# Turning q and k by DMA transposes in SBUF instead of TensorE transposes and bank copies, in a windowed attention followed by a mixture of experts

## The chip, the cores and the metric

The kernel runs on one core of one Trainium2 chip. The metric is the device time of one execution in microseconds (us); less is better. A verdict needs 2%: faster, same or slower.

## The reference, cut to what matters

```python
# q, k, v: (4 batches, 8 heads, 768 tokens, 64), float32; n_sink = 4, window = 128
scores = scale * q @ k.T
keep = is_sink | ((rel >= 0) & (rel < window))      # first 4 keys, and the last 128
a = softmax(where(keep, scores, -1e9))
x = (a @ v) as (3072 tokens, 512)                   # 4 x 768 tokens, 8 heads x 64
# a mixture of 4 experts, dense: every token goes through every expert
p = domain_probs / sum(domain_probs)
out = sum over e of p[:, e] * (relu(x @ w1[e]) @ w2[e])   # 512 -> 1024 -> 512
```

## The kernel before

The expert products are most of the work. Attention of batch b+1 is woven into the expert products of batch b, by a small model of the engines' times that the kernel carries in its Python: it decides the program's order when the kernel is built. At run time TensorE keeps to that order: it stands before a step that has to wait, even with products behind it that are ready.

The score products of this kernel read q and k with the head dimension on the partitions (`sps<-qkT 64*128` in the page). Before, each batch is loaded with tokens on the partitions, cast to bf16 on the way, regrouped by head, turned by TensorE into a PSUM bank (12 transposes for a pair of heads), and copied out of the bank:

```python
def load_qk(b, piece):                       # one DMA each for q and k, T tokens per partition
    s0, T = PIECES[b][piece]
    ...
        nc.gpsimd.dma_start(out=x, in_=src[b, :, s0:s0 + P * T, :]
                            .rearrange("h (p t) d -> p h (t d)", t=T))   # T = 6: runs of 1536 bytes

def transposes(b, piece, hp, tag="mix"):
    ...
    for i, name in enumerate("qk"):
        for tt in range(T):
            nc.tensor.transpose(tr[:, i, tt], nat[b, piece, name][:, tt, 2 * hp:2 * hp + 2, :], ident)
    done = pe(2 * T * P, grouped[b, piece], free_at(tag))
    engine, at = sooner(2 * T * P, done, rate=0.9)
    copy(engine, qkT[b, hp][:, :, s0:s0 + T * P].rearrange("c i (p t) -> c i p t", t=T),
         tr.rearrange("c i t p -> c i p t"))
    ...
```

The main loop starts the next batch's attention when the present one is done. `load_w1(3)` and `load_w2(3)` bring the last expert's weights, 1 MB each as written:

```python
        if not att.more() and ahead + 1 < B and (ahead == 0 or mix.done >= cols * ahead):
            ahead += 1
            load_qk(ahead, 0)
            load_v(ahead, range(NQB))
            if ahead == 1:
                load_w1(3)
                load_w2(3)
            att = Attention(ahead, [("regroup", ahead, 0, 0)]
                + [("transposes", ahead, 0, hp) for hp in range(NHP)]
                + [("sinks", ahead, 0, 0)], range(NG))
```

`sinks` is the first step that reads the turned q and k: GpSimd makes the sink keys (`ksd`) from the turned k, then TensorE multiplies them with the turned q.

The softmax here doesn't subtract the row's maximum and nothing guards it: scores larger than these inputs give would overflow.

Of the kernel before, what the change touches and what calls it, by code (L numbers as in the profile page):

```python
# [12 lines left out]
BF16 = mybir.dt.bfloat16  # L13
# [3 lines left out]
def kernel(  # L17
# [12 lines left out]
    nc = tc.nc  # L30

    B, H, S, D = q.shape
    NSINK = int(n_sink)
# [4 lines left out]
    P = 128  # L38
# [6 lines left out]
    NQB = S // P  # L45
    NHP = H // 2
# [28 lines left out]
    def act(cols, *deps):  # L75
        t["act"] = max(t["act"], *deps) + 190 + cols / 1.2
        return t["act"] + 60

    def dve(cols, *deps, rate=0.96):
        t["dve"] = max(t["dve"], *deps) + 130 + cols / rate  # L80
        return t["dve"] + 60
# [12 lines left out]
    def lands(key, nbytes):  # L94
        dma["at"] += nbytes / 350.0
        landed[key] = dma["at"] + 1500
# [9 lines left out]



    nat = {}

    def load_qk(b, piece):
        s0, T = PIECES[b][piece]
        for name, src in (("q", q), ("k", k)):
            x = sb.tile([P, H, T * D], BF16, name=f"{name}n", tag=f"{name}n", bufs=1)
            nc.gpsimd.dma_start(
                out=x, in_=src[b, :, s0:s0 + P * T, :].rearrange("h (p t) d -> p h (t d)", t=T),
            )
            nat[b, piece, name] = x
        lands(("qk", b, piece), 2 * H * P * T * D * 4)

    def load_first():

# [11 lines left out]
    def copy(engine, out, in_):  # L134
        (nc.scalar.copy if engine == "act" else nc.vector.tensor_copy)(out=out, in_=in_)  # L135

    def sooner(cols, *deps, rate=0.96):

        a = max(t["act"], *deps) + 190 + cols / 1.2
        d = max(t["dve"], *deps) + 130 + cols / rate  # L140
        if a <= d:
            return "act", act(cols, *deps)
        return "dve", dve(cols, *deps, rate=rate)
# [134 lines left out]
        for _ in range(n):  # L278
            nc.tensor.matmul(x[:, 0:cols], lhsT=zeros[:, 0:P], rhs=zeros[:, 0:cols], start=True, stop=True)

    qkT, xT, sinkA, aTs, onats = {}, {}, {}, {}, {}
    turned_at, sinkA_at, aT_at, onat_at, xT_at = {}, {}, {}, {}, {}

    def two_banks(tag="mix"):

# [5 lines left out]
    def transposes(b, piece, hp, tag="mix"):  # L291

        s0, T = PIECES[b][piece]
        if (b, hp) not in qkT:
            qkT[b, hp] = sb.tile([P, 2, S], BF16, name="qkT", tag="qkT", bufs=5)
        tr = psum.tile([P, 2, T, P], BF16, name="tr", tag=tag, bufs=1 if tag == "mix" else 2)
        for i, name in enumerate("qk"):
            for tt in range(T):
                nc.tensor.transpose(tr[:, i, tt], nat[b, piece, name][:, tt, 2 * hp:2 * hp + 2, :], ident)  # L299
        done = pe(2 * T * P, grouped[b, piece], free_at(tag))  # L300
        engine, at = sooner(2 * T * P, done, rate=0.9)
        copy(
            engine, qkT[b, hp][:, :, s0:s0 + T * P].rearrange("c i (p t) -> c i p t", t=T),
            tr.rearrange("c i t p -> c i p t"),
        )
        take(tag, at)
        turned_at[b, piece, hp] = at

    def sink_keys(b):
        for hp in range(NHP):  # L310
            nc.gpsimd.tensor_mul(  # L311
                ksd[b % 2][:, hp, 0:2 * NSINK].rearrange("p (a j) -> p a j", a=2),
                qkT[b, hp][:, 1, None, 0:NSINK].to_broadcast([P, 2, NSINK]),
                half[:, :, None].to_broadcast([P, 2, NSINK]),
            )

    def sink_values(b):
        nc.gpsimd.tensor_mul(
            vsd[:, b], vsf[:, b, None, None, :].to_broadcast([P, NHP, 2, DX]), sel2,
        )  # L320

    def sinks(b, piece):

        if b not in sinkA:
            sinkA[b] = sb.tile([P, 2 * G], BF16, name="sinkA", tag="sinkA", bufs=2)
        s0, T = PIECES[b][piece]
        q0, q1 = max(G, s0), s0 + T * P
        sp, _ = two_banks()
        for hp in range(NHP):
            nc.tensor.matmul(  # L330
                sp[0][32 * hp:32 * hp + 32, 0:q1 - q0], lhsT=ksd[b % 2][:, hp, :],
                rhs=qkT[b, hp][:, 0, q0:q1], start=True, stop=True,
            )
        nc.scalar.activation(
            out=sinkA[b][:, q0 - G:q1 - G], in_=sp[0][:, 0:q1 - q0], func=AF.Exp, scale=scale,
        )
        done = pe(q1 - q0 + 300, free_at("mix"), *[turned_at[b, piece, hp] for hp in range(NHP)])
        at = act(q1 - q0, done)
        take("mix", at)
        for g in range(q0 // G, q1 // G):  # L340
            sinkA_at[b, g] = at

    def scores(b, hp, g, tag="mix"):
        T = qkT[b, hp]
        w = sum(x[2] for x in GROUPS[g]) * P
        sps, both = two_banks(tag)
        c = 0
        for (kb, qb, nq) in GROUPS[g]:
            for ph in range(2):
                pr = slice(64 * ph, 64 * ph + 64)  # L350
                nc.tensor.matmul(  # L351
                    sps[ph][:, c:c + nq * P],
                    lhsT=T[pr, 1, kb * P:(kb + 1) * P],
                    rhs=T[pr, 0, qb * P:(qb + nq) * P],
                    start=True, stop=True,
                )
            c += nq * P
        done = pe(1.5 * w, scores_ready(b, hp, g, tag))
        a = sb.tile([P, 2, w], BF16, name="aT", tag="aT", bufs=4)
        m = mask0 if g == 0 else mask1  # L360
        if both is not None:
            nc.scalar.activation(out=a, in_=both[:, :, 0:w], func=AF.Exp, scale=scale)  # L362
            nc.vector.tensor_mul(a, a, m[:, None, :].to_broadcast([P, 2, w]))  # L363
            at = act(2 * w, done)
            take(tag, at)
            at = dve(2 * w, at, rate=1.9)
        else:
            for ph in range(2):
                nc.scalar.activation(out=a[:, ph], in_=sps[ph][:, 0:w], func=AF.Exp, scale=scale)
                nc.vector.tensor_mul(a[:, ph], a[:, ph], m)  # L370
                at = act(w, done)
                take(tag, at)
                at = dve(w, at, rate=1.9)
        aTs[b, hp, g], aT_at[b, hp, g] = a, at
# [64 lines left out]
    class Attention:  # L439
# [29 lines left out]
        def emit(self, step):  # L469
            self.steps += 1  # L470
            if step == "turn":
                turn(*self.valued.pop(0))
            elif step == "values":
                u = self.scored.pop(0)
                values(*u)
                self.valued.append(u)
            else:
                kind, b, x, y = self.todo.pop(0)
                if kind == "scores":
                    scores(b, x, y)  # L480
                    self.scored.append((b, x, y))
                elif kind == "regroup":
                    regroup(b, x)
                    if b > 0:
                        sink_values(b)
                elif kind == "transposes":
                    transposes(b, x, y)
                elif kind == "sinks":
                    if b > 0:
                        sink_keys(b)  # L490
                    sinks(b, x)


# [147 lines left out]
    while mix.more() or att.more():  # L641
        now = t["pe"]

        if not att.more() and ahead + 1 < B and (ahead == 0 or mix.done >= cols * ahead):
            ahead += 1
            load_qk(ahead, 0)
            load_v(ahead, range(NQB))
            if ahead == 1:
                load_w1(3)
                load_w2(3)  # L650
            att = Attention(
                ahead, [("regroup", ahead, 0, 0)] + [("transposes", ahead, 0, hp) for hp in range(NHP)]
                + [("sinks", ahead, 0, 0)], range(NG),
            )
            upto = mix.done
        share = (cols * ahead - upto) * 0.96
        due = ahead == 0 or att.steps * share <= (mix.done - upto) * att.total
        opts = []
        if att.more():
            opts = [(max(r, now), 0 if due else 3, "att", step) for r, step in att.options()]  # L660
        f, s2 = mix.first_ready(), mix.second_ready()
        opts.append((max(f, now), 2, "first", None))
        opts.append((max(s2, now), 1 if mix.since >= 2 else 2.5, "second", None))
        r, _, kind, step = min(opts, key=lambda o: (o[0] > now + 40, o[0] if o[0] > now + 40 else 0, o[1]))
        if kind == "att":
            att.emit(step)
        elif kind == "first":
            mix.emit_first()
        else:
            mix.emit_second()  # L670
# [35 lines left out]
```

## Time and profile before

| | before |
|---|---|
| time, median of the first three runs | 420.56 us (419.39 to 420.58) |
| span of the profiled run | 417.9 us |
| TensorE busy | 398.6 us, 95% |
| ScalarE / VectorE busy | 188.7 us / 176.0 us |
| TensorE transposes of q and k | 192 |

The page of the kernel before: each engine's busy time with its share of the span and its instructions, then the span in 40 slices (10.4 us each, busy tenths; PEclk is the granted TensorE clock in tenths).

```profile
PE 398.6 (95%) x2874; PEld 229.3 (55%) x2918; DVE 176.0 (42%) x349; ACT 188.7 (45%) x336; POOL 50.1 (12%) x94
...
PE   6598899999999999999999999999999999999996
...
PEclk9599899999999999999999999999999999999999
DMA  9999999292011129200002100000001100000012
```

TensorE is full from the sixth slice on. All its holes lie in the first five, in batch 0's attention, and so does its half clock, but for the last of it, which ends at 53.4 us. Whatever is taken from TensorE after that should shorten the kernel by as much (e8 below tests it).

What one group of 12 transposes costs is read from the timeline of TensorE before (start in us, length, engine, line, operation, operands, count). The lengths overlap (68.53 + 0.50 lies past the next start, 68.87), so starts count: from 68.53 to the next product's 69.20 it is 0.67 us.

```profile
68.53 0.50 PE L299 MATMUL tr<-ident,qo 128*128 128x128 bf16 x6
68.87 0.50 PE L299 MATMUL tr<-ident,ko 128*128 128x128 bf16 x6
69.20 2.15 PE L547 MATMUL hps<-xT,w 128*128 128x256 bf16 x16
```

The hole at the end of batch 0's attention, and the first long run of expert products after it, in the timeline of TensorE before:

```profile
48.92 0.29 PE L402 MATMUL od<-vx,aT 128*128 128x65 bf16 x4 [1.33 <-DVE aT L363]
...
50.39 6.10 PE L547 MATMUL hps<-xT,w 128*128 128x256 bf16 x36
```

Two windows of 1 us of the kernel before (columns: length, then busy time and instructions of PE, PEld, DVE, ACT, POOL; clock; DMA share; GB/s written). In the first, q and k are read in runs of 1536 bytes, in the second v in runs of 256. (These are float32 in HBM; cast to bf16 they are written as packets of 768 and 128 bytes.)

```profile
86.00:87.00 1.00, 1.00 (x14) 0.60 (x13) 0.26 (x1) 0.15 (x1) 1.00 (x2) 1.00 1.33 199
...
92.00:93.00 1.00, 0.95 (x6) 0.41 (x6) 0.46 (x3) 0.95 (x2) 0.00 (x0) 1.00 2.43 155
```

### The profile page before, as it was taken

What the parts mean: (1) busy time and instruction counts of PE and PEld (TensorE: products, weight loads), DVE (VectorE), ACT (ScalarE), POOL (GpSimd) and SP (SyncE); (2) the same over time, 40 slices, a digit from 0 to 9 for tenths busy, and PEclk for the clock granted to TensorE, in tenths of its full rate; (3) what the DMA queues carried; (4) which work ended last, traced back from release to release, by engine and by line L of the source; (5) the groups of instructions that cost most, each with busy time, mean ns of one, the idle gap of its engine ahead of it and who ended that gap; (6) DMA issues with size and microseconds to landing.
All of it is one profiled execution on the core that took longest, in us unless ns stands there. A gap on an engine that the chain in (4) does not pass through costs nothing.

```text
span 417.9 us, 7002 instructions
## 1 busy us (share of the span) xinstructions
PE 398.6 (95%) x2874; PEld 229.3 (55%) x2918; DVE 176.0 (42%) x349; ACT 188.7 (45%) x336; POOL 50.1 (12%) x94
## 2 busy tenths in 40 slices
PE   6598899999999999999999999999999999999996
PEld 2366566666676555555555555555555555555552
DVE  3666655565564446343333444334334222222222
ACT  3556315473641554445544645355534333333331
POOL 8745120440000044000000000000000000000000
PEclk9599899999999999999999999999999999999999
DMA  9999999292011129200002100000001100000012
GB/s 175 191 194 209 206 182 164 28 184 17 2 41 61 52 28 184 18 0 2 0 2 77 76 2 0 2 0 2 2 0 56 72 27 0 2 0 2 0 51 100
DMA packets 47428, 25.16 MB, mean 60 GB/s; under 512 B 29965, under 2 KB 42253, under 8 KB 47397
## 3 DMA queue, kind: packets, MB, share of 16 engines
q0 software_dynamic: 41632, 17.30, 33.4%
q1 hardware_dynamic: 5764, 7.42, 5.1%
q8 instruction: 22, 0.36, 0.3%
q14 instruction: 10, 0.07, 0.1%
HBM read 35.73 MB, written 6.29 MB: 101 GB/s over the span
## 4 chain that ended last, share of the span: by engine, by line
PE 91%; DMA 3%; ACT 2%; POOL 1%; DVE 1%; issue 1%; ACTq 0%
PE hps L547 41%; PE mop L582 39%; PE sps L351 3%; DMA kn<-in_k_dram 3%; PE tr L299 3%; PE od L402 2%; PE tx L427 1%; ACT aT L362 1%; PE od L395 1%; POOL vx L177 0%; ACT qkT L135 0%; DVE ht L558 0%; PE sps L330 0%; DVE aT L363 0%; ACT ko L135 0%
## 5 line engine op out<-in xcount | busy, mean ns | idle before, releaser
L547 PE MATMUL hps<-xT,w 128*128 128x384 bf16 (+1 forms) x1152 | 195.6, 310 | 0.5
L582 PE MATMUL mop<-w,ht 128*128 128x512 bf16 x724 | 174.5, 379 | 3.3 <-issue 1.4
L556 ACT ACTIVATE ht<-hps 128x384 bf16<-128x384 f32 (+1 forms) x222 | 103.0, 470 | 149.3 <-PE hps L547 148.3
L547 PEld LDWEIGHTS <-w 128*128 128x128 bf16 x1152 | 108.2, 98 | 62.3 <-issue 8.4
L582 PEld LDWEIGHTS <-ht 128*128 128x128 bf16 x768 | 73.0, 98 | 77.8 <-issue 2.7
L592 DVE SCALAR_TENSOR_TENSOR out_sb<-mop,scale_t,out_sb 128x512 f32<-128x512 f32 x72 | 54.0, 750 | 106.9 <-PE mop L582 105.8
L363 DVE TENSOR_TENSOR aT<-aT,mask 128x1024 bf16<-128x1024 bf16 (+1 forms) x46 | 31.2, 678 | 50.9 <-ACT aT L362 50.7
L362 ACT ACTIVATE aT<-sps 128x1024 bf16<-128x1024 f32 (+1 forms) x46 | 44.0, 957 | 12.6 <-PE sps L351 12.4
L558 DVE TENSOR_SCALAR ht<-hps 128x256 bf16<-128x256 f32 (+1 forms) x66 | 29.8, 451 | 18.9 <-PE hps L547 16.9
L590 DVE TENSOR_SCALAR out_sb<-mop,scale_t 128x512 f32<-128x512 f32 x24 | 18.0, 750 | 34.9 <-PE mop L582 34.8
L135 ACT COPY qkT<-tr 128x1536 bf16<-128x1536 bf16 (+1 forms) x20 | 21.9, 1098 | 16.5 <-PE tr L299 16.5
L135 ACT COPY xT<-tx 128x256 bf16<-128x256 bf16 x32 | 11.9, 374 | 26.6 <-PE tx L427 26.0
L311 POOL TENSOR_TENSOR ksd<-qkT,half 128x8 bf16<-128x8 bf16 x16 | 3.1, 203 | 170.0 <-ACT qkT L135 170.0
L402 PE MATMUL od<-vx,aT 128*128 128x65 bf16 x352 | 20.9, 197 | 2.4 <-DVE aT L363 2.4
L177 POOL DMA_DIRECT2D vx<-in_v_dram x24 | 21.3, 915 | 9.8 <-DMA w<-in_moe_w_dram 9.8
L402 PEld LDWEIGHTS <-aT 128*128 128x128 bf16 x352 | 17.8, 100 | 6.8 <-DVE aT L363 3.2
L412 DVE TENSOR_TENSOR onat<-od,R 128x256 bf16<-128x256 f32 x48 | 20.4, 424 | 1.7
L351 PE MATMUL sps<-qkT 64*128 64x128 bf16 (+1 forms) x256 | 18.4, 246 | 0.5
L427 PE MATMUL tx<-ident,onat 128*128 128x128 bf16 x96 | 13.7, 228 | 3.7 <-DVE onat L412 3.0
L427 PEld LDWEIGHTS <-onat 128*128 128x128 bf16 x96 | 8.3, 99 | 11.5 <-DVE onat L412 4.7
L351 PEld LDWEIGHTS <-qkT 64*128 64x128 bf16 x256 | 8.0, 96 | 10.9 <-issue 9.1
L395 PE MATMUL od<-vsd,sinkA 128*128 128x130 bf16 x64 | 12.9, 220 | 0.0
(60 smaller groups left out, 119.4 us busy)
## 6 DMA issues: line engine op xcount, KB each, us to landing
w<-in_moe_w_dram POOLq DMA_DIRECT2D x8, 1024.0 KB, 15.3
out_dram<-out_sb SPq DMA_DIRECT2D x24, 256.0 KB
vx<-in_v_dram POOLq DMA_DIRECT2D x24, 128.0 KB, 10.9
qn<-in_q_dram POOLq DMA_DIRECT2D x3, 768.0 KB, 7.8
kn<-in_k_dram POOLq DMA_DIRECT2D x3, 768.0 KB, 10.9
qraw<-in_q_dram SPq DMA_DIRECT2D x2, 256.0 KB
kraw<-in_k_dram SPq DMA_DIRECT2D x2, 256.0 KB
qn<-in_q_dram POOLq DMA_DIRECT2D x2, 256.0 KB, 9.9
```

The source lines that it names most:

```text
L135: (nc.scalar.copy if engine == "act" else nc.vector.tensor_copy)(out=out, in_=in_)
L177: nc.gpsimd.dma_start(out=vx[b % 2][:, tb, :, 0:D], in_=v[b, :, tb * P:(tb + 1) * P, :].rearrange("h p d -> p h d"),)
L351: nc.tensor.matmul(sps[ph][:, c:c + nq * P], lhsT=T[pr, 1, kb * P:(kb + 1) * P], rhs=T[pr, 0, qb * P:(qb + nq) * P], start=True, stop=True,)
L362: nc.scalar.activation(out=a, in_=both[:, :, 0:w], func=AF.Exp, scale=scale)
L363: nc.vector.tensor_mul(a, a, m[:, None, :].to_broadcast([P, 2, w]))
L402: nc.tensor.matmul(od[:, qi, ph], lhsT=a[:, ph, c:c + P], rhs=vx[b % 2][:, kb, 2 * hp + ph, 0:DX], start=(g == 0 and i == 0), stop=(i == l ...
L427: nc.tensor.transpose(tx[:, qi], o[:, qi], ident)
L547: nc.tensor.matmul(hp_, lhsT=w1_sb[e][:, db, fb * P:(fb + 1) * P], rhs=xT[b, db][:, t0:t0 + n], start=(db == 0), stop=(db == NDB - 1),)
L556: nc.scalar.activation(out=ht, in_=hp_, func=AF.Relu)
L558: nc.vector.tensor_scalar(out=ht, in0=hp_, scalar1=0.0, scalar2=None, op0=ALU.max)
L582: nc.tensor.matmul(op, lhsT=hts[fb][:, off:off + P], rhs=w2_sb[e][:, fb, :], start=(fb == 0), stop=(fb == NFB - 1),)
L592: nc.vector.scalar_tensor_tensor(out=dst, in0=op, scalar=sc, in1=dst, op0=ALU.mult, op1=ALU.add,)
```

## The change

The intent is to take 144 transposes off TensorE, and 12 bank copies and the regroupings of batches 1 to 3 off ScalarE and VectorE, by giving the turning to the DMA engines, which are mostly idle after the first 70 us (31 of the last 33 slices of the page before show 0 to 2 tenths). q and k of these batches are loaded by blocks of 128 tokens (six loads each), and one DMA transpose each writes them turned into SBUF. Batch 0 keeps TensorE, but its turned q and k move to the new layout, and each bank copy is split over ScalarE and VectorE. The diff, cut to its core (the uses of `qkT[b, hp]` become uses of `qkT[b][..., hp, :]`):

```diff
+    def load_rows(b):
+        for i, (name, src) in enumerate((("q", q), ("k", k))):
+            x = sb.tile([P, NQB, H, D], BF16, name=f"{name}n", tag=f"{name}n", bufs=1)
+            for tb in range(NQB):
+                nc.gpsimd.dma_start(
+                    out=x[:, tb], in_=src[b, :, tb * P:(tb + 1) * P, :].rearrange("h p d -> p h d"),
+                )
+                lands(("rows", b), H * P * D * 4)
+            if b not in qkT:
+                qkT[b] = sb.tile([P, 2, NQB, NHP, P], BF16, name="qkT", tag="qkT", bufs=2)
+            nc.sync.dma_start_transpose(
+                out=qkT[b][:, i].rearrange("c t h p -> c (t h) p"),
+                in_=x.rearrange("p t h d -> p (t h d)"),
+            )
+        for hp in range(NHP):
+            turned_at[b, 0, hp] = max(landed["rows", b], t["pe"]) + 11000.0
...
     def transposes(b, piece, hp, tag="mix"):            # batch 0 only, now
-        engine, at = sooner(2 * T * P, done, rate=0.9)
-        copy(engine, qkT[b, hp][:, :, s0:s0 + T * P]..., tr...)
+        for i, engine in enumerate(("act", "dve")):
+            copy(engine, qkT[b][:, i, s0 // P:s0 // P + T, hp, :]..., tr[:, i]...)
+        at = max(act(T * P, done), dve(T * P, done, rate=0.9))
...
-            load_qk(ahead, 0)
+            load_rows(ahead)
             load_v(ahead, range(NQB))
             if ahead == 1:
                 load_w1(3)
                 load_w2(3)
             att = Attention(
-                ahead, [("regroup", ahead, 0, 0)] + [("transposes", ahead, 0, hp) for hp in range(NHP)]
-                + [("sinks", ahead, 0, 0)], range(NG),
+                ahead, [("sinks", ahead, 0, 0)], range(NG),
             )
```

The 11000 is nanoseconds: where the scheduler's model expects the transposes to be done. It places TensorE's sink scores in the program, it does not make anything wait less.

More of the change, by code (lines that the diff above doesn't have):

```diff
@@ L105 @@
     ctx.enter_context(tc.manual_schedule())
-    nat = {}
+    nat, qkT, turned_at = {}, {}, {}
     def load_qk(b, piece):
@@ L279, in idle_products @@
             nc.tensor.matmul(x[:, 0:cols], lhsT=zeros[:, 0:P], rhs=zeros[:, 0:cols], start=True, stop=True)
-    qkT, xT, sinkA, aTs, onats = {}, {}, {}, {}, {}
-    turned_at, sinkA_at, aT_at, onat_at, xT_at = {}, {}, {}, {}, {}
+    xT, sinkA, aTs, onats = {}, {}, {}, {}
+    sinkA_at, aT_at, onat_at, xT_at = {}, {}, {}, {}
     def two_banks(tag="mix"):
@@ L293, in transposes @@
         s0, T = PIECES[b][piece]
-        if (b, hp) not in qkT:
-            qkT[b, hp] = sb.tile([P, 2, S], BF16, name="qkT", tag="qkT", bufs=5)
+        if b not in qkT:
+            qkT[b] = sb.tile([P, 2, NQB, NHP, P], BF16, name="qkT", tag="qkT", bufs=2)
         tr = psum.tile([P, 2, T, P], BF16, name="tr", tag=tag, bufs=1 if tag == "mix" else 2)
@@ L300, in transposes @@
         done = pe(2 * T * P, grouped[b, piece], free_at(tag))
-        engine, at = sooner(2 * T * P, done, rate=0.9)
-        copy(
-            engine, qkT[b, hp][:, :, s0:s0 + T * P].rearrange("c i (p t) -> c i p t", t=T),
-            tr.rearrange("c i t p -> c i p t"),
-        )
+        for i, engine in enumerate(("act", "dve")):
+            copy(
+                engine, qkT[b][:, i, s0 // P:s0 // P + T, hp, :].rearrange("c n (p t) -> c n p t", t=T),
+                tr[:, i].rearrange("c t (n p) -> c n p t", n=T),
+            )
+        at = max(act(T * P, done), dve(T * P, done, rate=0.9))
         take(tag, at)
@@ L312, in sink_keys @@
                 ksd[b % 2][:, hp, 0:2 * NSINK].rearrange("p (a j) -> p a j", a=2),
-                qkT[b, hp][:, 1, None, 0:NSINK].to_broadcast([P, 2, NSINK]),
+                qkT[b][:, 1, 0, hp, None, 0:NSINK].to_broadcast([P, 2, NSINK]),
                 half[:, :, None].to_broadcast([P, 2, NSINK]),
@@ L331, in sinks @@
                 sp[0][32 * hp:32 * hp + 32, 0:q1 - q0], lhsT=ksd[b % 2][:, hp, :],
-                rhs=qkT[b, hp][:, 0, q0:q1], start=True, stop=True,
+                rhs=qkT[b][:, 0, q0 // P:q1 // P, hp, :], start=True, stop=True,
             )
@@ L343, in scores @@
     def scores(b, hp, g, tag="mix"):
-        T = qkT[b, hp]
+        T = qkT[b]
         w = sum(x[2] for x in GROUPS[g]) * P
@@ L352, in scores @@
                     sps[ph][:, c:c + nq * P],
-                    lhsT=T[pr, 1, kb * P:(kb + 1) * P],
-                    rhs=T[pr, 0, qb * P:(qb + nq) * P],
+                    lhsT=T[pr, 1, kb, hp, :],
+                    rhs=T[pr, 0, qb:qb + nq, hp, :],
                     start=True, stop=True,
@@ L483, in emit @@
                     regroup(b, x)
-                    if b > 0:
-                        sink_values(b)
                 elif kind == "transposes":
@@ L490, in emit @@
                         sink_keys(b)
+                        sink_values(b)
                     sinks(b, x)
```

## The prediction

> **What bounds the kernel now.** TensorE. The busy table has it at 398.6 of 417.9 us (95%), and the chain of waits runs 91% through its instructions. From about 56 us on it practically never waits; its idle time (the 40 slices and a table of 2 us windows) lies before that, in batch 0's attention, where it also runs at half clock from about 9 to 22.5 us and, after a hole at 47.4 to 50.2 us, from 50 to 53.4 us. ScalarE (45%) and VectorE (42%) are no limits after that.
>
> **What goes, what comes.** For batches 1 to 3 the change removes:
> - TensorE: 12 groups of 12 transposes. In the timeline one group takes 0.67 us from its start to the next product's start (68.53 to 69.20, 149.75 to 150.42): 12 x 0.67 = 8.0 us, all on the path, since TensorE is saturated there.
> - ScalarE: 12 bank copies of 1.44 us, and the regroupings on ScalarE and VectorE: about 25 us of engine time, worth almost nothing.
>
> It adds, per batch, 12 loads with 256-byte runs in place of two with 1536-byte runs. The 1 us windows show v, with such short runs, at 155 GB/s written (91 to 94 us), against 200 to 206 for q and k (84 to 89): 1.57 MB takes an estimated 10.1 us in place of 7.8. For batches 2 and 3 this happens a whole batch ahead (loads issue at 80 and 153 us): free. For batch 1 the weights in front end near 49.7 us, so k should land near 61 us; what needs it stands near 75 us in the new order.
>
> It adds two DMA transposes of 786 KB per batch, in the SP queue behind output stores. For batches 2 and 3 they cannot start before the fifth store of the former batch, and the new order puts the sink scores that need them only about 10 us of TensorE work later. [...] TensorE waits 0 to 2 us at batches 2 and 3, none at batch 1.
>
> Batch 0 keeps its transposes, but each copy is split over ScalarE and VectorE (0.59 or 0.69 us become an estimated 0.4 us on both); each bank then waits for both in-order engines, and the third piece's transposes move later. I count +0.5 us.
>
> **Sum.** 420.6 - 8.0 + 0.5 + about 0.4 of waits: **413.5 us**, 80% range **409.5 to 422**. Chances: faster by over 2% 0.30, within 2% 0.58, slower 0.12.
>
> **What would show it.** Transposes on TensorE 192 -> 48, its busy time down by about 8 us, ScalarE's by about 20 us; no wait of the sink scores over 2 us; SP's queue with six transposes whose pairs land 8 to 11 us after issue; q and k loaded at about 155 GB/s; TensorE still saturated from 56 us on.
>
> **What would make it wrong.** DMA transposes much slower than 200 GB/s: TensorE, in order, then stands at the sink scores of batches 2 and 3, each hole costing its length and some 1.7 us of half clock after it (as after the hole at 47 us)[...]. Or batch 1's loads or transposes slowed by the v and w loads around them. Or the hole at 47 us going with the new order of batch 0: 2 us better.

The sum came to 413.5 us, with the four terms that it shows. The 200 GB/s of the last paragraph are a condition of the forecast; measured were 200 to 206 GB/s for the loads of q and k before, and 270 for a transpose alone.

## The result, and the profile after

| | before | after |
|---|---|---|
| time, median of 4 runs | 420.25 us | 431.92 us (430.65 to 432.80) |
| ratio | | 1.028 (1.025 to 1.031): slower |
| span of the profiled run | 417.9 us | 431.1 us |
| TensorE / ScalarE busy | 398.6 / 188.7 us | 398.3 / 169.4 us |

The same lines of the page, after (slices of 10.8 us):

```profile
PE 398.3 (92%) x2774; PEld 223.2 (52%) x2774; DVE 168.1 (39%) x348; ACT 169.4 (39%) x331; POOL 76.0 (18%) x124
...
PE   7599799049999999999999999999999999999996
...
PEclk9599889759999999999999999999999999999999
DMA  9999999999800159910000180000001110000012
```

There is a new hole in the eighth and ninth slice with half clock behind it, and the DMA engines are busy through it. Everything later is full. The waits of TensorE after (who waited for whom: total us, times, longest) name it, and GpSimd's own wait says what stood behind it:

```profile
PE sps L349 <- POOL ksd L330: 15.7, 1, 15.7
...
POOL ksd L330 <- DMA qkT<-kn: 162.5, 3, 77.7
```

It is one wait: of three batches with DMA transposes, one has it. (GpSimd's 162.5 us are harmless; it has nothing else to do.) The timeline of TensorE after shows where:

```profile
51.75 6.80 PE L565 MATMUL hps<-xT,w 128*128 128x256 bf16 x36
...
74.98 1.04 PE L565 MATMUL hps<-xT,w 128*128 128x256 bf16 x8
91.70 1.08 PE L349 MATMUL sps<-qkT,ksd 128*32 128x512 bf16 x4 [15.69 <-POOL ksd L330]
92.71 3.59 PE L600 MATMUL mop<-w,ht 128*128 128x512 bf16 x8
```

The sink scores of batch 1 stood at 76 us in the program, as predicted, and ran at 91.70. The eight products after them took 3.59 us in place of 1.89: half clock. The timeline of the SP queue after has the six transposes (the length is the time that SP was held by issuing it; the output stores between the pairs are left out):

```profile
54.92 7.41 SPq L132 DMA_TRANSPOSE qkT<-qn  x1
62.57 15.10 SPq L132 DMA_TRANSPOSE qkT<-kn  x1
...
155.86 3.04 SPq L132 DMA_TRANSPOSE qkT<-qn  x1
159.13 3.06 SPq L132 DMA_TRANSPOSE qkT<-kn  x1
...
250.87 3.10 SPq L132 DMA_TRANSPOSE qkT<-qn  x1
254.21 2.93 SPq L132 DMA_TRANSPOSE qkT<-kn  x1
```

The same instruction took 2.9 to 3.1 us to issue at batches 2 and 3 and 7.4 and 15.1 us at batch 1, and what lay behind it in the queue waited: a store whose data was ready at 158.17 us was issued at 162.29, after batch 2's pair. In the chain of waits after (start, length, what), the stretch before the hole is one transfer:

```profile
62.57 28.74 DMA qkT<-kn
```

The trace also has every DMA packet with its queue, start and size. Counted in stretches of 2 us, q0 being the loads issued by GpSimd and q1 the transposes (256-byte packets, 3072 for q and as many for k):

```
kernel after            q0 loads                        q1 transposes
60 to 62 us    255 x 128 B                              927 x 256 B  119 GB/s
68 to 70 us    1081 x 128 B                             560 x 256 B   72 GB/s
74 to 76 us    132 x 128 B and 44 x 2048 B              174 x 256 B   22 GB/s
82 to 84 us    39 x 1024 B and 82 x 2048 B              124 x 256 B   16 GB/s
158 to 159 us (1 us, batch 2)   none                   1132 x 256 B  290 GB/s
```

In the five stretches from 80 to 90 us, beside packets of 1024 and 2048 bytes only, the transposes moved 16 to 34 GB/s. By its packets, k of batch 1 was turned from 68.0 to 90.9 us: 22.8 us. k of batch 2, with no load beside it, took 2.9 us (160.3 to 163.2). And the last expert's weights suffered in return: their packets run from 71.5 to 93.9 us, against 59.9 to 72.0 us before.

Three reasons could stand behind this:
- **A**: the long packets of the weight loads, beside which the transposes starve.
- **B**: the short packets of v and of the late q and k rows; the weights do not matter.
- **C**: the first DMA transposes of a program are slow by themselves.

And a second, smaller loss was there before the hole: the run of 36 expert products starts at 51.75 us in place of 50.39 and takes 6.80 us in place of 6.10, at half clock for 6.8 us in place of 3.4.

### The profile page after: what moved, and what is told of

Its sections match the earlier page's. It is cut to its first block, busy times and chain, and to the rows that moved or that the text cites. A ratio compares the mean times of both kernels' runs of the same rounds, so it can differ in the third digit from the quotient of the medians. Undisturbed runs are those within 1.5% of the kernel's fastest.

```text
span 431.1 us, 6810 instructions
## 1 busy us (share of the span) xinstructions
PE 398.3 (92%) x2774; PEld 223.2 (52%) x2774; DVE 168.1 (39%) x348; ACT 169.4 (39%) x331; POOL 76.0 (18%) x124
## 4 chain that ended last, share of the span: by engine, by line
PE 77%; DMA 17%; POOL 4%; DVE 0%; issue 0%; ACT 0%; ACTq 0%; DVEq 0%; POOLq 0%
PE mop L600 36%; PE hps L565 35%; DMA w<-in_moe_w_dram 9%; DMA qkT<-kn 7%; PE sps L370 3%; PE od L421 2%; POOL vx L195 2%; DMA vx<-in_v_dram 1%; POOL kn L126 1%; PE tx L446 1%; PE od L414 1%; PE sps L349 0%; DVE ht L576 0%; POOL kn L115 0%; POOL qn L115 0%
## 5 line engine op out<-in xcount | busy, mean ns | idle before, releaser
L574 ACT ACTIVATE ht<-hps 128x384 bf16<-128x384 f32 (+1 forms) x234 | 109.2, 471 | 188.5 <-PE hps L565 187.2
L600 PE MATMUL mop<-w,ht 128*128 128x512 bf16 x768 | 183.0, 382 | 0.0
L565 PEld LDWEIGHTS <-w 128*128 128x128 bf16 x1152 | 109.4, 99 | 66.5 <-issue 9.4
L382 DVE TENSOR_TENSOR aT<-aT,mask 128x1024 bf16<-128x1024 bf16 (+1 forms) x46 | 30.0, 652 | 39.8 <-ACT aT L381 39.5
L330 POOL TENSOR_TENSOR ksd<-qkT,half 128x8 bf16<-128x8 bf16 x16 | 2.7, 196 | 162.5 <-DMA qkT<-kn 162.5
L576 DVE TENSOR_SCALAR ht<-hps 128x256 bf16<-128x256 f32 (+1 forms) x54 | 23.1, 429 | 11.1 <-PE hps L565 9.3
L126 POOL DMA_DIRECT2D qn<-in_q_dram x18 | 15.9, 904 | 10.0 <-DVE R L428 8.1
L126 POOL DMA_DIRECT2D kn<-in_k_dram x18 | 15.9, 926 | 8.5 <-ACT aT L381 4.3
L349 PE MATMUL sps<-qkT,ksd 128*32 128x512 bf16 (+1 forms) x20 | 2.5, 390 | 15.7 <-POOL ksd L330 15.7
L153 ACT COPY xT<-tx 128x256 bf16<-128x256 bf16 x25 | 9.1, 373 | 16.6 <-PE tx L446 16.0
```

The lines of the kernel that those rows point to most:

```text
L126: nc.gpsimd.dma_start(out=x[:, tb], in_=src[b, :, tb * P:(tb + 1) * P, :].rearrange("h p d -> p h d"),)
L382: nc.vector.tensor_mul(a, a, m[:, None, :].to_broadcast([P, 2, w]))
L565: nc.tensor.matmul(hp_, lhsT=w1_sb[e][:, db, fb * P:(fb + 1) * P], rhs=xT[b, db][:, t0:t0 + n], start=(db == 0), stop=(db == NDB - 1),)
L574: nc.scalar.activation(out=ht, in_=hp_, func=AF.Relu)
L576: nc.vector.tensor_scalar(out=ht, in0=hp_, scalar1=0.0, scalar2=None, op0=ALU.max)
L600: nc.tensor.matmul(op, lhsT=hts[fb][:, off:off + P], rhs=w2_sb[e][:, fb, :], start=(fb == 0), stop=(fb == NFB - 1),)
```

## The experiments

All eight gave the reference's result. The first four shared one chip and seven runs of the kernel before (420.90 us), the other four another and seven runs (420.40 us).

### e1_w3_after: the last weights after the transposes

```diff
-            if ahead == 1:
-                load_w1(3)
-                load_w2(3)
...
                     if b > 0:
                         sink_keys(b)
                         sink_values(b)
+                    if b == 1:
+                        load_w1(3)
+                        load_w2(3)
```

> The changed kernel, but the last expert's two weight loads (2.1 MB written) are issued only once batch 1's transposes have landed. Theory A (the transposes of batch 1 share the DMA engines packet by packet with those weight loads, and starve): k's transpose of batch 1 lands before 72 us in place of 91 us, the 15.7 us wait of TensorE at batch 1's sink scores is under 1 us, and the time falls by that wait and the half clock behind it, about 18 to 19 us, to 413 us (411.5 to 415). Theory B (the short-run loads of k and v slow the transposes, the weights do not matter): k's transpose still lands after 80 us and at least 6 us of the wait stay: 420 or more. Theory C (the first transposes are slow by themselves, whatever runs beside them): nothing changes, 431 us.

Measured: 415.95 us (415.65 to 416.48), ratio 0.989 (0.987 to 0.991). TensorE's wait for the sink keys, in its waits of this run:

```profile
PE sps L349 <- POOL ksd L330: 0.3, 1, 0.3
```

k was turned by 75.7 us (its packets), not before 72 as A had it, as v's short packets still ran beside it until 73.8; but the wait is gone. B and C both asked for a wait that stays, so as they were stated they fall: without the weights there is no loss. The time came down by 16 us, of which the wait is 15.4. A's forecast of 413 missed by 3 us, though its saving came: from the 101st product of the first expert layer (in every kernel just after batch 0's attention) to the last one, TensorE needs 343.4 us in place of 361.4, 18.0 less. But e1 reaches that 101st product 0.9 us later than the changed kernel (60.97 against 60.11), for which no run shows the cause, and the changed kernel's profiled run, from which the wait was read, took 432.8 us, 0.9 more than its median.

### e2_v_first: v out of the way, the weights beside the transposes

```diff
-            load_rows(ahead)
-            load_v(ahead, range(NQB))
+            if ahead == 1:
+                load_v(ahead, range(NQB))
+                load_rows(ahead)
+            else:
+                load_rows(ahead)
+                load_v(ahead, range(NQB))
```

> The changed kernel, but batch 1's v is loaded before its q and k, so that v is out of the way when k is transposed and only the weight loads run beside it; q and k land about 5 us later. Theory A (weights): k's transpose still lands at 88 us or later and TensorE waits 10 us or more: 427 to 437 us. Theory B (v and the other short-run loads): the wait falls below 6 us and the time below 422 us.

Measured: 416.41 us (415.68 to 417.57), ratio 0.990. A said 427 to 437 and is wrong as well. B's forecast for this run (a wait under 6 us, a time under 422) is met, but e1 had already ruled B out:

```profile
PE sps L349 <- POOL ksd L330: 1.4, 1, 1.4
```

The packets say why. Beside the weights the transposes did starve, just as A has it: from 66 to 68 us 179 load packets, nearly all of 2048 bytes, and exactly 179 transpose packets, 23 GB/s. But the weights lost little: 181 GB/s in that stretch, and 14.8 us for all of them (62.2 to 77.0) against 12.1 before. Then the transposes ran at 274 GB/s and were done at 81.1. (The scheduler had also moved the sink scores about 4.5 us later, to 80.5 us, since it counts v's bytes as coming first. With the old place the wait would have been an estimated 6 us: 1.4 plus 4.5.) So neither kind of load alone makes the 15.7 us: with v alone (e1) k was turned at 75.7 us, with the weights alone at 81.1 (though the transposes began 5.8 us later there, at 64.0), with both at 90.9. That asks for a theory of what passes between the two queues; e7 tests one.

### e3_te_batch1: batch 1 turned by TensorE

```diff
+            if b == 1:                       # in load_rows: no DMA transpose
+                nat[b, 0, name] = x
+                continue
...
-                ahead, [("sinks", ahead, 0, 0)], range(NG),
+                ahead, ([("transposes", 1, 0, hp) for hp in range(NHP)] if ahead == 1 else [])
+                + [("sinks", ahead, 0, 0)], range(NG),
```

> The changed kernel with batch 1 alone turned by TensorE again (rows loaded as in the change, 48 transposes, bank copies split over two engines); batches 2 and 3 by DMA. If the loss is all in batch 1's hole (A and B alike), the hole and its half clock go (about 19 us) and 4 x 0.67 = 2.7 us of transposes return: 415.5 us (414 to 418). If the DMA transposes of batches 2 and 3 or batch 0's split copies cost much too, it stays above 420.

Measured: 417.59 us (416.92 to 418.32), ratio 0.993. It lies in the range. The DMA transposes of batches 2 and 3 are a gain, and the row loads (which this run keeps) are not the loss. It also speaks against C: here batch 2's are the first DMA transposes of the program, and by its packets the first of them took 3.1 us.

### e4_later_sinks: the same transfers, met later

```diff
-            turned_at[b, 0, hp] = max(landed["rows", b], t["pe"]) + 11000.0
+            turned_at[b, 0, hp] = max(landed["rows", b], t["pe"]) + (28000.0 if b == 1 else 11000.0)
```

> The changed kernel with one number of its scheduler changed: batch 1's turned q and k are expected 28 us after the load step in place of 11 us, so TensorE gets batch 0's expert products first and meets batch 1's sink scores near 92 us. If what costs is only TensorE standing in order before a late transpose, the wait falls below 3 us although the transpose lands as late as before (85 us or later): 413 to 416 us. If the slow transposes also hold back something else that TensorE needs (the last expert's weights, v), waits appear there instead and it stays above 420 us.

Measured: 415.14 us (413.99 to 415.39), ratio 0.987. Here the transfers are as slow as in the changed kernel (k turned at 90.3 us, the weights done at 94.2), but TensorE's timeline has the sink scores without a wait (the first line is GpSimd's, in its own timeline):

```profile
90.92 0.67 POOL L330 TENSOR_TENSOR ksd<-qkT,half 128x8 bf16<-128x8 bf16 x4 [29.21 <-DMA qkT<-kn]
...
92.60 0.40 PE L349 MATMUL sps<-qkT,ksd 128*32 128x512 bf16 x4
```

The slow transfers cost nothing that shows by themselves (e1, without them, took 415.95). What cost was TensorE, in order, standing in front of them while expert products that were ready lay behind in its program.

### e5_one_copy: e1 with batch 0's bank copies on one engine each

```diff
-        for i, engine in enumerate(("act", "dve")):
+        engine, at = sooner(2 * T * P, done, rate=0.9)
+        for i in range(2):
             copy(engine, qkT[b][:, i, s0 // P:s0 // P + T, hp, :]..., tr[:, i]...)
-        at = max(act(T * P, done), dve(T * P, done, rate=0.9))
```

> The run with the last weights after the transposes (415.95 us), with batch 0's bank copies each put back on one engine. In that run the 65th product of the first expert layer started at 52.4 us against 50.4 before, and half clock lasted 6.8 us from 51 us against 3.4. If the split copies made that, it starts at 50.5 to 51 us here and the time is 413.5 to 414.5 us. If the strided bank copies of the new layout or the row loads beside them made it, it stays at 415.5 to 416.5 us.

Measured: 413.99 us (413.40 to 414.52), ratio 0.985. The time is as the split copies' theory has it, 2.0 us under e1. The milestone is not: the 65th product starts at 51.5 us, not by 51. What did shrink is the half clock after it, 3.4 us again in place of 6.8 in this profile.

### e6_before_split: that part of the change alone

The kernel before, with nothing changed but batch 0's bank copies:

```diff
-        engine, at = sooner(2 * T * P, done, rate=0.9)
-        copy(engine, qkT[b, hp][:, :, s0:s0 + T * P]..., tr...)
+        if b == 0:
+            for i, engine in enumerate(("act", "dve")):
+                copy(engine, qkT[b, hp][:, i, s0:s0 + T * P]..., tr[:, i]...)
+            at = max(act(T * P, done), dve(T * P, done, rate=0.9))
+        else:
+            ...                              # as before
```

> The kernel before with one part of the change alone: batch 0's bank copies split over ScalarE and VectorE, in the old layout, and the order that the scheduler makes of it. If that part costs what the milestones say, 422 to 423 us (1.5 to 2.5 us over before). If it costs nothing, 420.3 to 421.2 us.

Measured: 421.88 us (421.75 to 422.45), ratio 1.0039 (1.0024 to 1.0054): 1.5 us over before, just under the forecast's 422. The split, with the order that the scheduler makes of it, costs about 1.5 to 2 us, and it does so without DMA transposes.

### e7_short_w3: the weights in short packets

```diff
-                load_w1(3)                   # one load, runs of 1024 elements
-                load_w2(3)                   # one load, runs of 512 elements
+                for c in range(0, F, 256):   # four loads, runs of 256 elements (512 bytes)
+                    nc.gpsimd.dma_start(out=w1_sb[3][:, :, c:c + 256], in_=...[:, :, c:c + 256])
+                for c in range(0, Dout, 256):    # two loads
+                    nc.gpsimd.dma_start(out=w2_sb[3][:, :, c:c + 256], in_=...[:, :, c:c + 256])
```

> The changed kernel with the last expert's weights loaded in runs of 512 bytes in place of 2048 and 1024 (six loads in place of two), in the same place of the queue, still after v. Theory D (packets take turns, so a 256-byte transpose packet gets an eighth of the bytes of a 2048-byte one beside it): the transposes move 60 GB/s or more beside these weights in place of 16 to 34, k lands at 82 us or before, and TensorE waits under 7 us: 416 to 423 us. Theory E (it is the mixture of three kinds of traffic in flight that collapses, whatever the length): k lands after 87 us and the wait stays over 11 us: 427 us or more.

Measured: 421.67 us (421.39 to 421.99), ratio 1.0032. The same bytes in the same place of the queue, cut into packets a quarter (w1) or half (w2) as long, and the wait of TensorE is under a third:

```profile
PE sps L349 <- POOL ksd L330: 4.7, 1, 4.7
```

k was turned at 80.5 us. From 78 to 80 us the trace has 449 packets of 512 bytes and 449 of 256: turn by turn, 115 and 57 GB/s. The turns can be seen one by one: packets of one kind start in a bunch of about 16, then as many of the other, and the pattern comes back every 67 ns. Landing, wait and time are as D has them, and E falls. (The rate was just under D's 60 GB/s there; from 76 to 78 us, where the traffic changes, it was 29.)

### e8_apart: nothing beside the transposes

The edits of e1, e2 and e5 together.

> Nothing beside batch 1's transposes: v before q and k, the last weights after the transposes, and batch 0's copies on one engine. If contention is all that slowed them, the two transposes land within 9 us of k's last load, as those of batches 2 and 3 do, TensorE waits under 1 us for them, and the time is 412.5 to 414.5 us: the saved 8.0 us of TensorE work less what is still lost in batch 0.

Measured: 413.18 us (412.85 to 413.63), ratio 0.983 (0.982 to 0.985): the best of all, better than both kernels, though short of 2%. The SP queue of this run, and the sink keys and sink scores in the timelines of GpSimd and TensorE:

```profile
60.97 5.76 SPq L132 DMA_TRANSPOSE qkT<-qn  x1
66.96 3.98 SPq L132 DMA_TRANSPOSE qkT<-kn  x1
...
73.01 0.67 POOL L330 TENSOR_TENSOR ksd<-qkT,half 128x8 bf16<-128x8 bf16 x4 [12.24 <-DMA qkT<-kn]
...
81.58 0.40 PE L349 MATMUL sps<-qkT,ksd 128*32 128x512 bf16 x4
```

k's packets end at 72.4 us; GpSimd made the sink keys at 73.0 us and TensorE came to them at 81.6 without a wait. C falls here too: by their packets the two transposes took 5.2 us (k's last rows still landed beside the first) and 4.2 us. That is slower than the 2.9 to 3.4 us of batches 2 and 3, which no run explains, but far from the 22.8 us of k in the changed kernel. In the same profile, from the 101st product of the first expert layer to the last, TensorE needs 342.7 us (59.15 to 401.80) against 350.4 before (58.05 to 408.47): 7.7 of the 8.0 us that the transposes were said to be worth. At the 101st product it is still 1.1 us behind. The new layout's two small copies for each large one may be the cause, or the clock: in this profile the first half-clock spell lasts 17.1 us against 13.7 before, and none follows the hole. No run parts the two.

## Why the prediction was wrong

- **TensorE bounds the kernel; 144 transposes are worth 8.0 us.** Right. e8 has 7.7 us of it. That TensorE's busy time would fall by 8 us did not show in the changed kernel (398.6 to 398.3), because products at half clock are busy for longer (eight took 3.59 us in place of 1.89), and because the trace before lacks 44 of 768 records of the second expert product; in two runs with all records it is 401.8 (e6, all transposes on TensorE) and 394.3 (e8).
- **ScalarE falls by about 20 us, worth nothing.** Right: 188.7 to 169.4.
- **Loads in 256-byte runs at 155 GB/s, k in near 61 us.** Right: 155 GB/s, and k's transpose was issued at 62.57.
- **A pair of transposes takes 8 to 11 us and just fits at batches 2 and 3.** Right: from the first issue to the sink keys 8.0 us (155.86 to 163.82) and 8.2 us (250.87 to 259.09), and no wait. Each transpose took 2.9 to 3.1 us by its packets (k of batch 2: 786 KB in 2.91 us, 270 GB/s).
- **"TensorE waits 0 to 2 us at batches 2 and 3, none at batch 1."** This step failed, in its second half. The prediction took one duration for all six transposes. At batch 1 they run beside v and the last expert's weights, q took 8.9 us and k 22.8 in place of the 2.9 to 3.1 us of batches 2 and 3, and TensorE waited 15.7 us. Behind it came half clock until 97.7 us: about 6 us of products at half speed, 3 us lost. The prediction named this ("batch 1's loads or transposes slowed by the v and w loads around them") among what could go wrong and put no number on it, although the timeline before already showed those loads issued right behind q and k.
- **Batch 0: +0.5 us.** Mis-sized: the split alone costs 1.5 us (e6) to 2.0 us (e1 against e5), and the changed kernel reaches the 101st product of the first expert layer 2.1 us later than before (60.11 against 58.05).

The sum with the measured terms, profile against profile: 417.9 - 7.7 + 2.1 + 15.7 + 3.0 = 431.0 us, against a span of 431.1 us after.

How the transposes starved: beside the weights, the DMA engines served the two queues in turns, packet for packet. The counts show this in e2 (179 to 179) and e7 (449 to 449), and e7 shows that the length of the other's packet set the transposes' share: 57 GB/s beside packets of 512 bytes, against 23 beside nearly all 2048 in e2. In e7's trace the kind changes after a bunch of about 16 packets, and a pair of bunches takes 67 ns: for the 16 engines of the page an estimated one packet of each kind per engine. At one packet of 256 bytes to one of 2048, the transposes had a ninth of the bytes moved (e2: 23 of 204 GB/s).

Beside v's packets of 128 bytes the turns are not one to one: 255 loads to 927 transposes from 60 to 62 us, and 1081 to 560 from 68 to 70. There the loads fell as well, from 155 GB/s to 16. What sets the shares there is not shown.

Why both kinds together were worse than either is not shown. From 74 to 76 us there were 176 load packets to 174 transpose packets, so the sixteen engines made an estimated 11 turns each, one in about 182 ns. That is close to a turn with a weight packet (179 ns in e2, where nearly every load packet had 2048 bytes), though by the counts (132 of 176) an estimated twelve of the engines still had v's 128 bytes. All three ran late: v's packets ended at 79.3 us against 61.9 before, the weights' at 93.9 against 72.0, and k's turning at 90.9. No run takes that apart.

The cost of the hole beyond its length: the half-clock spells last 3.4 us (before, from 49.9), 6.8 (after, from 50.0), 13.7 (both, from 9.0) and 17.1 us (after, from 80.7 in the hole to 97.7 behind it, and the first of e8). They are 1, 2, 4 and 5 times the shortest. What sets their start and length is not shown.

## What to carry to other kernels

When work moves from an engine to the DMA queues, cost it with the traffic that will be in flight at that moment: here, where packets took turns beside the weights, a transfer of 256-byte packets was an eighth as fast as its neighbour of 2048-byte ones (23 against 181 GB/s in e2). Before moving a transfer, list what is issued within its latency, and put the bulk loads that nothing needs soon behind it (here: 16 us for a move of two lines). A scheduler that fixes an engine's order, as this one does TensorE's, must place the first use by the slow case; placing it too late cost nothing here that shows (e4), too early cost 15.7 us.
